# Folding two of the first batch's three sample tiles on TensorE, in float32

## The chip, the cores and the metric

The kernel runs on one core of a Trainium2 chip. The metric is the time of one execution on the device, in microseconds (us). The engines of the core work side by side, each on its own stream of instructions: TensorE (PE in the profile; its weight loads are PEld), VectorE (DVE), ScalarE (ACT), GpSimd (POOL) and SyncE (SP), which here only starts transfers.

## The reference

A batch `x` of shape 4 x 3072 x 256 goes through a Fourier transform over both its axes, of which the real part is kept. Then follow a gated layer whose gate mixes the 3072 tokens with a 3072 x 3072 matrix, and a second gated layer.

```python
X = np.fft.fft(np.fft.fft(x, axis=1), axis=2)
x = X.real.astype(np.float32)
h = np.maximum(x @ w_in, 0.0)
u, v = h[..., :512], h[..., 512:]
v_n = (v - mean(v)) / np.sqrt(var(v) + 1e-06)
v_s = np.einsum('ts,bsd->btd', w_spatial, v_n) + b_spatial[None, :, None]
x = (u * v_s) @ w_out
gate = 1.0 / (1.0 + np.exp(-(x @ w_gate)))
return (gate * (x @ w_val)) @ moe2_w_out
```

## The kernel before, in words

Float32 accuracy is made of float32r matmuls: an operand is split into a high part (a cast on ScalarE) and a low part (a subtraction on VectorE), and `mm3` (lines 259 to 261) forms high x high, high x low and low x high, three matmuls for one product, and leaves low x low out.

The program has three stages. The first transforms the four batches one after the other and multiplies by `w_in`; the second is the large product with `w_spatial`, and the third the last layer. The order on every engine is written out by hand (`manual_schedule`): an engine gets its instructions in the order in which the Python code issues them.

The change is in what precedes the first batch's transform, the opening. There

- three sample tiles of batch 0 (m = 0, 1, 2), each in two halves `xt` of 512 KB (`xts[m, hd]`), are folded: rows that the transform's symmetry pairs are added and subtracted over three levels, from 16 x 64 values per partition down to 8 x 64. `fold_x` and `folds` (lines 356 to 379) do one half tile with twelve VectorE instructions. The result, `fo[m]`, is split into `fh` and `fl` (`split_fold`);
- `w_in` comes as 64-bit words in four pieces. `convert` makes float32 of two pieces at a time: `from64_first` on ScalarE (lines 275 and 276, two instructions a piece), `from64_rest` on VectorE (lines 281 to 299), a cast to `wih` on ScalarE (line 463), and, in the returned `rest`, the low part `wil` on VectorE (line 468);
- `first_weights` multiplies the converted pieces by the transform over the model dimension: 16 matmuls `psg`, the first on `wih`, the second on `wil`; `take` brings them to `gc` and `g3`;
- `mirror_samples` (lines 537 to 541) makes the samples `sps` of special rows: once for batch 0 and the last column, once for batches 1 to 3;
- `take_nyquist` (lines 581 and 582) makes `nts`, of which `own_samples` (line 599, ScalarE) makes `nt`, that the first unit's fourth matmul (line 628) needs.

In program order the opening is: fold tile 2; convert pieces 0 and 1; exchange rows of tile 2; fold half 0 of tile 0; `wil`; `first_weights(1)`; fold half 1 of tile 0; `mirror_samples` for batch 0; split tile 0; `take`; convert pieces 2 and 3; fold half 0 of tile 1; `wil`; `first_weights(0)`; transform of tiles 2 and 0; fold half 1 of tile 1; split tile 1; and the rest of the first unit. From there on GpSimd folds the tiles of batches 1 to 3 while TensorE works on the batch before.

Of the kernel before, what the change touches and what calls it, by code (L numbers as in the profile page):

```python
# [9 lines left out]
F32 = mybir.dt.float32  # L10
# [5 lines left out]
ALU = mybir.AluOpType  # L16
# [3 lines left out]
B, S, D = 4, 3072, 256  # L20
# [4 lines left out]
P = 128  # L25
# [112 lines left out]
def _masks():  # L138
    m = np.zeros((P, 3 + B), np.float32)
    for b in range(B):  # L140
        m[32 * b : 32 * b + 3, 3 + b] = 1.0
        m[32 * b + 2, 0] = -1.0
        m[32 * b + 1, 1] = -1.0
    m[64:68, 2] = -1.0
    return m
# [8 lines left out]
def _slots():  # L154
    r = _samples()
    rows = [r, 768 - r, 1536 - r, 768 + r, 3072 - r, 2304 + r, 1536 + r, 2304 - r]
    return np.stack(rows, 1) % S


def layouts(x, moe_w_in, moe_w_spatial, moe_b_spatial, moe_w_out, moe2_w_gate, moe2_w_val, moe2_w_out):  # L160
    tau = _token_order()
    slots = _slots()
    dup = [3, 4, 6, 7]

    def halves(xb):

        o = np.zeros(xb.shape[:-1] + (2, P), np.float32)
        o[..., 0, :] = xb[..., :P]
        o[..., 1, 1:] = xb[..., : D // 2 : -1]
        return o  # L170

    g = x[:, slots]
    g[:, 0, dup] = 0.0
    xh = halves(g).reshape(B, 3, P, 8, 2, 2, 64).transpose(0, 1, 5, 2, 3, 4, 6)
    gn = g[..., D // 2].reshape(B, 3, P, 8).transpose(2, 3, 1, 0)
    fam = np.array([384, 1152, 1920, 2688])
    sp = halves(x[:, fam])
    xs = np.zeros((P, B + 1, 2, P), np.float32)
    for at in (0, 32, 64):
        xs[at : at + 4, :B] = sp.transpose(1, 0, 2, 3)  # L180
        for b in range(B):
            for c in range(3):
                xs[at : at + 4, B, 0, 32 * b + c] = x[b, fam, D // 2]
    w = moe_w_spatial[tau][:, tau]
    wt = w.reshape(6, 512, 24, P).transpose(0, 3, 2, 1)
    wg, wv = (w.reshape(2, P, 12, P) for w in (moe2_w_gate, moe2_w_val))
    arrays = {
        "xh": xh,
        "xn": gn.reshape(P, 8, 3 * B),
        "xs": xs,  # L190
        "w_in": moe_w_in.reshape(2, P, DFF).transpose(1, 0, 2),
        "wt": wt,
        "bt": moe_b_spatial[tau].reshape(1, S),
        "w_out": moe_w_out.reshape(4, P, DM).transpose(1, 0, 2).reshape(P, 2, 512),

        "w_b": np.concatenate(
            [
                np.stack([wg[0], wg[1], wv[1], wv[0]]).transpose(1, 2, 0, 3).reshape(P, 12, 512),
                moe2_w_out.reshape(12, P, DM).transpose(1, 0, 2).reshape(P, 6, 512),
            ],  # L200
            axis=1,
        ),
    }
    arrays.update(_constants())
    arrays["spc"] = _special_constants()
    arrays["fd"] = _dft_d()
    arrays["masks"] = _masks()

    arrays = {k: np.ascontiguousarray(v) for k, v in arrays.items()}
    return {k: v.view(np.uint64) if v.dtype == np.float64 else v for k, v in arrays.items()}, tau  # L210
# [27 lines left out]
def tile_kernel(ctx: ExitStack, tc: tile.TileContext, t: dict, out: bass.AP):  # L238
    nc = tc.nc
# [62 lines left out]
    def pool(stack, name, bufs, side="left", **kw):  # L302
        return stack.enter_context(tc.tile_pool(name=name, bufs=bufs, side=side, reuse_waits="tile", **kw))
# [4 lines left out]
    ln_all = lnp.tile([P, 320], F32, name="ln_all")  # L308
# [12 lines left out]
    ps_w = pool(ps0, "ps_w", 6, space=PSUM)  # L321
# [48 lines left out]
    def load_x(b, m, hd, p=xp, bufs=2):  # L370
        xt = p.tile([P, 8, 2, 64], F32, tag="xt", name="xt", bufs=bufs)
        nc.sync.dma_start(xt, t["xh"][b, m, hd])
        return xt

    def fold_x(eng, xt, fo, hd, et):
        at = slice(hd * 64, hd * 64 + 64)
        eng.tensor_tensor(out=et, in0=xt[:, :, 0, :], in1=xt[:, :, 1, :], op=ALU.add)  # L377
        eng.tensor_tensor(out=xt[:, :, 0, :], in0=xt[:, :, 0, :], in1=xt[:, :, 1, :], op=ALU.subtract)  # L378
        folds(eng, [(0, et, fo[:, 0, :, at]), (1, xt[:, :, 0, :], fo[:, 1, :, at])])

    def new_fo():
        return fop.tile([P, 2, 4, P], F32, tag="fo", name="fo")

    def new_et(p=xp):
        return p.tile([P, 8, 64], F32, tag="et", name="et", bufs=1)
# [15 lines left out]
    def fft(fold, b, unit, q, e=0, ps=None, tiles=(0, 1, 2), end=True, early=False):  # L401

        n = R3 if unit == 3 and q == 0 else H
        begin = ps is None
        if begin:

            ps = ps_w.tile([P, 512], F32, tag="pa", name="psf") if early else ps_f.tile([P, 512], F32, tag="f", name="psf")
        ops = []
        if unit < 2:
            for i, (m, s) in enumerate(((e, q), (e, 1 - q), (2, (e + q) % 2))):
                ops.append((m, s, [c[:, e, i, :] for c in cc["c1"]]))
        else:
            name = ("c2", "c3")[unit - 2] + "pq"[q]
            for m in range(3):
                ops.append((m, unit, [cc[name][i][:, m, :] for i in range(2)]))
        sp = {(0, 0): SP_P1, (0, 1): SP_Q1, (2, 1): SP_Q2, (3, 0): SP_P3}.get((unit, q)) if begin else None  # L420
        for i in tiles:
            m, s, c = ops[i]
            fh, fl = fold[m][:2]
            last = end and sp is None and i == tiles[-1]
            mm3(ps[:, :n], (fh[:, q, s, :], fl[:, q, s, :]), c, begin and i == tiles[0], last, skip_group_check=e > 0)
        if sp is not None:
            nc.tensor.matmul(out=ps[:, :n], lhsT=sps[:, b, q, :], rhs=spc[:, sp : sp + n], start=False, stop=end)
        return ps, n
# [16 lines left out]
    fo = {m: new_fo() for m in (2, 0, 1)}  # L445
    xts = {}
# [7 lines left out]
    def convert(two):  # L454

        new = lambda: tmp.tile([P, 512], F32, tag="cv", name="cv", bufs=5)
        values = from64_rest(from64_first([words[i] for i in two], new), new())
        parts = []
        for i, value in zip(two, values):
            c, h = pieces[i]  # L460
            sl = slice(h * 512, h * 512 + 512)
            hi, lo = (x[:, c, sl] for x in wih)
            nc.scalar.copy(hi, value)
            parts.append((hi, lo, value))

        def rest():
            for hi, lo, value in parts:
                nc.vector.tensor_tensor(out=lo, in0=value, in1=f(hi), op=ALU.subtract)

        return rest  # L470

    def fold0(m, hd):
        fold_x(nc.vector, xts[m, hd], fo[m], hd, new_et())


    xts[2, 0] = load_x(0, 2, 0)
# [1 line left out]
    words = [load_w(0), load_w(1)]  # L478
    xts[0, 0] = load_x(0, 0, 0)
    xts[0, 1] = load_x(0, 0, 1, tmp, RING)  # L480
    fd = tmp.tile([P, 2 * 512 + 256], F32R, name="fd")
    nc.gpsimd.dma_start(fd, t["fd"])
    xn = tmp.tile([P, 8, 3 * B], F32, name="xn")
# [11 lines left out]
    fold0(2, 1)  # L495
    xts[1, 0] = load_x(0, 1, 0)
    xts[1, 1] = load_x(0, 1, 1, tmp, RING)
    rest = convert([0, 1])
    words += [load_w(2), load_w(3)]
    fold = {2: split_fold(fo[2], 2, None)}  # L500
    fold0(0, 0)
    rest()

    def first_weights(h):
# [24 lines left out]
        return take  # L529

    take = first_weights(1)
    fold0(0, 1)

    es = tmp.tile([P, B + 1, P], F32, name="es")

    def mirror_samples(bs):
        nc.vector.tensor_tensor(out=es[:, bs], in0=xs[:, bs, 0, :], in1=xs[:, bs, 1, :], op=ALU.add)
        nc.vector.tensor_tensor(out=xs[:, bs, 1, :], in0=xs[:, bs, 0, :], in1=xs[:, bs, 1, :], op=ALU.subtract)
        for q, e in ((0, es[:, bs]), (1, xs[:, bs, 1, :])):
            nc.scalar.copy(sps[:, bs, q, :], e)  # L540
            nc.vector.scalar_tensor_tensor(
                out=sps[:, bs, q, :], in0=f(sps[:, bs, q, :]), scalar=masks[:, 2:3], in1=e, op0=ALU.mult, op1=ALU.add
            )
# [16 lines left out]
        nc.vector.tensor_tensor(out=lo, in0=src, in1=f(hi), op=ALU.subtract)  # L560
        fold_n[m] = (hl[:, 0:1], hl[:, 1:2])

    fold0(1, 0)
    rest()
    load_table("c2", {"c2p": (3, H), "c2q": (3, H)})
    take = first_weights(0)
    sums = [fft(fold, 0, 3, q, tiles=(2, 0), end=False, early=True) for q in range(2)]
    fold0(1, 1)
    spread(2)
    spread(0)  # L570
    fold[1] = split_fold(fo[1], 1)
# [3 lines left out]
    spread(1)  # L575
    pq = [take_fft(*sums[q], q) for q in range(2)]
    load_table("c1", {"c1": (2, 3, H)})
    mirror_samples(slice(1, B))

    def take_nyquist(ps, n, unit):  # L580
        nc.scalar.copy(nts[unit], ps[:, :n])
        nc.vector.scalar_tensor_tensor(
            out=nts[unit], in0=f(nts[unit]), scalar=masks[:, 0:1], in1=ps[:, :n], op0=ALU.mult, op1=ALU.add
        )

    for unit in (3, 2):
        take_nyquist(*fft(fold_n, B, unit, 0, early=True), unit)
    s0.close()
    stp = pool(r0, "stp", 2, "right")
    vp = pool(r0, "vp", 9, "right")  # L590
# [540 lines left out]
    p, i, c = leaves[-1]  # L1131
# [83 lines left out]
    for n, leaf in enumerate(leaves[:-1]):  # L1215
        p, i, c = leaf
        base = 4 * (n % 2)
        ps = [banks(base + d) for d in range(4)]
# [33 lines left out]
    ps = [banks(base + d) for d in range(4)]  # L1252
# [196 lines left out]
```

## Time and profile before

| | |
|---|---|
| time, median of 3 runs | 2888.73 us (2887.54 to 2888.93) |
| the profiled execution's own time | 2888.82 us |
| its span, first to last instruction | 2886.7 us |
| mean granted TensorE clock | 0.995 |
| TensorE busy | 2823.3 us (98% of the span) |
| VectorE busy | 2018.2 us (70%) |

The profile is that of one execution. The span leaves out some 2 us of the execution's own time. TensorE's share of busy time is an average: it says nothing of the opening, in which TensorE mostly waits.

### The profile page before, as it was taken

How to read it: one execution, taken by the hardware profiler on the slowest of the kernel's cores; microseconds unless marked ns; L12 is line 12 of the kernel's file. 1: busy time of each engine (PE TensorE's matmuls, PEld its weight loads, DVE VectorE, ACT ScalarE, POOL GpSimd, SP SyncE). 2: the span in 40 equal slices, each digit the busy share in tenths (PEclk: the TensorE clock that was granted, in tenths of full speed). 3: DMA queues.
4: the chain of work that ended last, by engine and by line, in shares of the span. 5: the costliest groups of instructions: out<-in, count | busy, mean ns of one | idle time of the engine just before them, and what ended most of it. 6: DMA issues, size and time to landing. Idle time of an engine off the chain costs nothing.

```text
span 2886.7 us, 34266 instructions
## 1 busy us (share of the span) xinstructions
PE 2823.3 (98%) x12550; PEld 2349.2 (81%) x12550; DVE 2018.2 (70%) x3001; ACT 1426.1 (49%) x2267; POOL 212.1 (7%) x333
## 2 busy tenths in 40 slices
PE   4999999999999999999999999999999999999999
PEld 4888788888888888888888888888888888888887
DVE  7777766797766567578667476866676666776665
ACT  4777444244334244344334333656556565565655
POOL 2883000001000000000000000000000000000000
PEclk9999999999999999999999999999999999999999
DMA  6777867798666678478776474200000000000000
GB/s 232 281 274 273 293 212 236 257 316 275 237 210 224 225 249 289 159 268 286 251 245 241 155 275 144 87 30 30 30 15 15 30 30 30 15 15 30 30 15 15
DMA packets 148180, 470.76 MB, mean 163 GB/s; under 512 B 16797, under 2 KB 18333, under 8 KB 147628
## 3 DMA queue, kind: packets, MB, share of 16 engines
q1 hardware_dynamic: 140540, 434.88, 43.9%
q0 software_dynamic: 4016, 21.11, 1.9%
q10 hardware_dynamic: 3456, 12.58, 1.1%
q8 instruction: 98, 1.61, 0.2%
q14 instruction: 70, 0.57, 0.1%
HBM read 385.94 MB, written 82.58 MB: 162 GB/s over the span
## 4 chain that ended last, share of the span: by engine, by line
PE 91%; POOL 3%; DVE 2%; ACT 1%; issue 1%; DMA 1%; ACTq 0%; SPq 0%; POOLq 0%; DVEq 0%
PE bank L259 30%; PE bank L260 30%; PE bank L261 30%; POOL et L377 0%; POOL xt L378 0%; DMA xt<-in_xh 0%; POOL fo L362 0%; POOL xt L360 0%; PE psf L259 0%; DMA u_d<-tu 0%; PE psv L260 0%; PE psv L259 0%; PE psv L261 0%; PE psu L261 0%; PE psu L260 0%
## 5 line engine op out<-in xcount | busy, mean ns | idle before, releaser
L259 PE MATMUL bank<-wh,vh 128*128 128x512 f32 x2016 | 785.7, 390 | 5.7 <-DVE ln_all L708 5.7
L261 PE MATMUL bank<-wh,vl 128*128 128x512 f32 x2016 | 785.5, 390 | 0.0
L260 PE MATMUL bank<-wl,vh 128*128 128x512 f32 x2016 | 785.4, 390 | 0.0
L828 ACT CAST wh<-st 128x1024 fp32r<-128x1024 f32 x252 | 264.4, 1049 | 507.1 <-PE bank L261 389.0
L831 DVE TENSOR_TENSOR wl<-st,wh 128x1024 fp32r<-128x1024 f32 x252 | 309.7, 1229 | 235.5 <-ACT wh L828 230.6
L259 PEld LDWEIGHTS bank<-wh,vh 128*128 128x128 f32 x2016 | 379.2, 188 | 85.2 <-DVE ln_all L708 6.4
L261 PEld LDWEIGHTS bank<-wh,vl 128*128 128x128 f32 x2016 | 379.1, 188 | 79.0
L260 PEld LDWEIGHTS bank<-wl,vh 128*128 128x128 f32 x2016 | 379.2, 188 | 78.6
L259 PE MATMUL bank<-x,wgh 128*128 128x512 f32 x673 | 262.4, 390 | 0.5 <-ACT t L1344 0.4
L1332 DVE TENSOR_TENSOR t<-t,bank 128x512 f32<-128x512 f32 x144 | 99.0, 688 | 233.7 <-PE bank L261 233.7
L260 PE MATMUL bank<-x,wgh 128*128 128x512 f32 x673 | 261.8, 389 | 0.0
L261 PE MATMUL bank<-x,wgl 128*128 128x512 f32 x673 | 261.8, 389 | 0.0
L1353 DVE TENSOR_TENSOR gl<-s,gh 128x512 fp32r<-128x512 f32 x288 | 199.5, 693 | 57.7 <-ACT gh L1351 44.3
L259 PE MATMUL bank<-gh,wv 128*128 128x512 f32 x576 | 224.2, 389 | 0.8 <-ACT gh L1346 0.8
L260 PE MATMUL bank<-gl,wv 128*128 128x512 f32 x576 | 224.2, 389 | 0.2 <-DVE gl L1353 0.2
L261 PE MATMUL bank<-gh,wv 128*128 128x512 f32 x576 | 224.1, 389 | 0.0
L826 DVE TENSOR_TENSOR st<-st 128x1024 f32<-128x1024 f32 x180 | 220.7, 1226 | 3.4 <-DMA st<-in_wt 3.1
L1323 ACT ACTIVATE s<-s 128x512 f32<-128x512 f32 x144 | 91.0, 632 | 153.1 <-DVE s L1322 153.1
L809 ACT ACTIVATE st<-st,ln_all 128x512 f32<-128x512 f32 x168 | 127.6, 808 | 66.3 <-DMA st<-v_d 52.4
L259 PEld LDWEIGHTS bank<-x,wgh 128*128 128x128 f32 x673 | 126.3, 188 | 28.6 <-ACT s L1320 0.9
L261 PEld LDWEIGHTS bank<-x,wgl 128*128 128x128 f32 x673 | 126.3, 188 | 26.2
L260 PEld LDWEIGHTS bank<-x,wgh 128*128 128x128 f32 x673 | 126.3, 188 | 26.0
(236 smaller groups left out, 4467.5 us busy)
## 6 DMA issues: line engine op xcount, KB each, us to landing
st<-in_wt SPq DMA_DIRECT2D x432, 512.0 KB, 5.4
st<-v_d SPq DMA_DIRECT2D x144, 512.0 KB, 5.3
u<-u_d SPq DMA_DIRECT2D x96, 256.0 KB, 3.5
u_d<-tu SPq DMA_DIRECT2D x48, 384.0 KB, 3.7
v_d<-tv SPq DMA_DIRECT2D x69, 256.0 KB, 3.7
xt<-in_xh SPq DMA_DIRECT2D x24, 512.0 KB, 4.1
x_d<-x ACTq DMA_DIRECT2D x24, 512.0 KB, 6.1
raw<-x_d SPq DMA_DIRECT2D x24, 512.0 KB, 4.0
```

What stands on the lines that cost most here:

```text
L259: nc.tensor.matmul(out=ps, lhsT=w[0], rhs=x[0], start=first, stop=False, **kw)
L260: nc.tensor.matmul(out=ps, lhsT=w[0], rhs=x[1], start=False, stop=False, **kw)
L261: nc.tensor.matmul(out=ps, lhsT=w[1], rhs=x[0], start=False, stop=last, **kw)
L809: nc.scalar.activation(st[:, k, :], st[:, k, :], AF.Identity, scale=scale[:, at], bias=shift[:, at])
L826: nc.vector.tensor_tensor(out=tiles[0], in0=tiles[0], in1=tiles[1], op=op)
L828: nc.scalar.copy(hl[0], tiles[0])
L831: lows.append(lambda: nc.vector.tensor_tensor(out=hl[1], in0=tiles[0], in1=f(hl[0]), op=ALU.subtract))
L1323: nc.scalar.activation(s1, s1, AF.Sigmoid)
L1332: nc.vector.tensor_tensor(out=g["t2"], in0=g["t2"], in1=g["b"], op=ALU.add)
L1353: nc.vector.tensor_tensor(out=l, in0=s, in1=f(h), op=ALU.subtract)
```

## The change

Tiles 0 and 1 of batch 0 are no longer folded by `fold_x`. `fold0_sums` has TensorE add the rows: for each half tile 8 matmuls in float32, of 256 columns each, with the identity or its negative as weights and `xt` as it came (not split) as the moving operand. They form the first two additions of the fold, in two PSUM tiles `psx`. ScalarE copies half of each of them to `fo`. `fold0_rest` does the remaining levels with six VectorE instructions of 128 x 256 for the whole tile. The identity and its negative are a new input of 128 KB, loaded by ScalarE's own DMA queue into `ln_all`, which is not yet in use then. `mirror_samples` for batches 1 to 3 moves behind `take_nyquist`.

```diff
+    arrays["ident"] = np.concatenate([np.eye(P), -np.eye(P)], 1).astype(np.float32)
...
+    ident = ln_all[:, : 2 * P]
+    signs = {0: ((1, 1), (1, 1)), 1: ((1, -1), (-1, 1))}
...
+    def fold0_sums(m):
+
+        sums = [ps_w.tile([P, 4, P], F32, tag="pa", name="psx") for _ in range(2)]
+        for hd in range(2):
+            xt = xts[m, hd]
+            for q, ps in enumerate(sums):
+                terms = [(half, k) for half in range(2) for k in range(2)]
+                for half, k in terms:
+                    w = ident[:, :P] if signs[q][half][k] > 0 else ident[:, P:]
+                    nc.tensor.matmul(
+                        out=ps[:, :, hd * 64 : hd * 64 + 64],
+                        lhsT=w,
+                        rhs=xt[:, 4 * half : 4 * half + 4, k, :],
+                        start=(half, k) == (0, 0),
+                        stop=(half, k) == (1, 1),
+                        skip_group_check=hd > 0,
+                    )
+        for q, ps in enumerate(sums):
+            nc.scalar.copy(fo[m][:, q, 2:4, :], ps[:, 2:4, :])
+        return sums
+
+    def fold0_rest(m, sums):
+
+        tt = nc.vector.tensor_tensor
+        e = new_et().rearrange("p s d -> p (s d)").rearrange("p (q s d) -> p q s d", q=2, s=2)
+        for q, ps in enumerate(sums):
+            plus, minus = (e[:, q], fo[m][:, q, 0:2, :])[:: -1 if q else 1]
+            tt(out=plus, in0=ps[:, 0:2, :], in1=fo[m][:, q, 2:4, :], op=ALU.add)
+            tt(out=minus, in0=ps[:, 0:2, :], in1=fo[m][:, q, 2:4, :], op=ALU.subtract)
+        to = fo[m].rearrange("p q s d -> p (q s) d")
+        tt(out=to[:, 2:8:5, :], in0=e[:, :, 0, :], in1=e[:, :, 1, :], op=ALU.subtract)
+        tt(out=to[:, 3:7:3, :], in0=e[:, :, 0, :], in1=e[:, :, 1, :], op=ALU.add)
...
+    nc.scalar.dma_start(ident, t["ident"])
     fd = tmp.tile([P, 2 * 512 + 256], F32R, name="fd")
...
+    sums = fold0_sums(0)
     rest = convert([0, 1])
     words += [load_w(2), load_w(3)]
     fold = {2: split_fold(fo[2], 2, None)}
-    fold0(0, 0)
+    fold0_rest(0, sums)
     rest()
...
     take = first_weights(1)
-    fold0(0, 1)
+    sums = fold0_sums(1)
...
-    fold0(1, 0)
+    fold0_rest(1, sums)
     rest()
...
-    fold0(1, 1)
     spread(2)
...
-    mirror_samples(slice(1, B))
...
     for unit in (3, 2):
         take_nyquist(*fft(fold_n, B, unit, 0, early=True), unit)
+    mirror_samples(slice(1, B))
     s0.close()
```

Line numbers of the kernel after are one higher than before up to line 470, and 38 or 39 higher behind that.

ScalarE at the start of the program, before (in brackets what an instruction waits for, an engine or a DMA queue):

```order
L275 ACT_TABLE_LOAD
L275 ACTIVATE cv<-words 128x512 [waits DMAHW2_49]
L276 ACTIVATE cv<-words 128x512
L275 ACTIVATE cv<-words 128x512 [waits DMAHW3_49]
L276 ACTIVATE cv<-words 128x512
L463 CAST wih<-cv 128x512 [waits DVE_49] x2
```

The same place after:

```order
L518 DMA ln_all<-in_ident 128x256
L497 ACT_TABLE_LOAD
L497 COPY fo<-psx 128x256 [waits PE_49] x2
L276 ACTIVATE cv<-words 128x512 [waits DMAHW3_49]
L277 ACTIVATE cv<-words 128x512
L276 ACTIVATE cv<-words 128x512 [waits DMAHW4_49]
L277 ACTIVATE cv<-words 128x512
L464 CAST wih<-cv 128x512 [waits DVE_49] x2
```

The two copies of tile 0's sums, which wait for TensorE, now stand ahead of the first conversion of `w_in`.

ScalarE behind the cast of tile 2, before:

```order
L396 CAST fh<-fo 128x1024 [waits Activation_49]
L540 CAST sps<-es 128x2x128 [waits DVE_49]
L540 CAST sps<-xs 128x2x128 [waits DMAHW0_49,DVE_49]
L254 CAST fh<-fo 128x1024
L521 CAST gh<-psg 128x512 [waits PE_49] x2
```

The same place after:

```order
L397 CAST fh<-fo 128x1024 [waits Activation_49]
L497 COPY fo<-psx 128x256 [waits PE_49] x2
L579 CAST sps<-es 128x2x128 [waits DVE_49]
L579 CAST sps<-xs 128x2x128 [waits DMAHW1_49,DVE_49]
L255 CAST fh<-fo 128x1024
```

The copies of tile 1's sums stand ahead of the samples `sps`, of tile 0's cast and of `take`; on TensorE these sums stand between `first_weights(1)` and `first_weights(0)`.

ScalarE at the end of the opening, before:

```order
L434 CAST ph<-psf 128x384 [waits PE_49]
L540 CAST sps<-es 128x3x128 [waits DVE_49]
L540 CAST sps<-xs 128x3x128 [waits DVE_49]
L581 CAST nt_144<-psf 128x386 [waits PE_49]
L581 CAST nt_143<-psf 128x384 [waits PE_49]
L599 ACTIVATE nt<-nt_144,masks 128x386 [waits DMAHW6_49,DMAHW7_49,DMASW0_49,DVE_49]
```

The same place after:

```order
L435 CAST ph<-psf 128x384 [waits PE_49]
L618 CAST nt_144<-psf 128x386 [waits PE_49]
L618 CAST nt_143<-psf 128x384 [waits PE_49]
L579 CAST sps<-es 128x3x128 [waits DVE_49]
L579 CAST sps<-xs 128x3x128 [waits DVE_49]
L637 ACTIVATE nt<-nt_144,masks 128x386 [waits DMAHW0_49,DMAHW7_49,DMASW0_49,DVE_49]
```

The samples of batches 1 to 3 have moved behind the two casts of `nts`; they still stand ahead of `nt`.

## Rows read from the trace of the kernel before

**Rows 1.** The page's first part: busy time, share of the span, instructions.

```profile
PE 2823.3 (98%) x12550; PEld 2349.2 (81%) x12550; DVE 2018.2 (70%) x3001; ACT 1426.1 (49%) x2267; POOL 212.1 (7%) x333
```

**Rows 2.** Stretch, length, busy PE, PEld, DVE, ACT, POOL; granted clock, DMA share, GB/s.

```profile
0.00:17.40 17.40, 0.00 (x0) 0.00 (x0) 12.65 (x37) 4.34 (x6) 4.64 (x12) 1.00 0.92 339
17.40:53.20 35.80, 18.41 (x70) 15.04 (x71) 34.41 (x84) 15.32 (x33) 8.33 (x10) 0.81 0.61 235
53.20:249.00 195.80, 184.34 (x934) 165.55 (x934) 143.40 (x392) 150.55 (x314) 148.03 (x233) 1.00 0.72 255
249.00:298.80 49.80, 38.01 (x177) 32.77 (x175) 38.42 (x109) 35.81 (x71) 17.24 (x32) 0.88 0.84 318
298.80:2886.70 2587.90, 2582.54 (x11373) 2135.84 (x11373) 1789.33 (x2383) 1220.05 (x1846) 33.87 (x48) 1.00 0.44 151
```

**Rows 3.** The chain that ended last, in the opening: start, duration, piece.

```profile
0.75 3.73 DMA xt<-in_xh
...
26.51 0.95 ACT fh L254
```

**Rows 4.** Timeline of VectorE: start, duration, line, operation, [idle before, releaser].

```profile
11.21 0.75 DVE L281 TENSOR_SCALAR cv<-cv 128x512 f32<-128x512 f32 x2
11.88 0.75 DVE L284 TENSOR_SCALAR cv<-cv 128x512 uint32<-128x512 uint32 x2
...
17.30 0.68 DVE L377 TENSOR_TENSOR et<-xt 128x512 f32<-128x512 f32 x1
...
18.63 0.42 DVE L360 TENSOR_TENSOR et<-et 128x256 f32<-128x256 f32 x1
18.96 0.42 DVE L360 TENSOR_TENSOR xt<-xt 128x256 f32<-128x256 f32 x1
...
20.65 1.28 DVE L468 TENSOR_TENSOR wil<-cv,wih 128x512 fp32r<-128x512 f32 x2
```

**Rows 5.** Timeline of ScalarE.

```profile
8.91 0.67 ACT L275 ACTIVATE cv<-words 128x512 f32<-128x512 f32 x1 [6.89 <-DMA words<-in_w_in]
9.48 0.66 ACT L276 ACTIVATE cv<-words 128x512 f32<-128x512 uint32 x1
10.57 0.67 ACT L275 ACTIVATE cv<-words 128x512 f32<-128x512 f32 x1 [0.42 <-DMA words<-in_w_in]
...
25.65 0.41 ACT L540 CAST sps<-es 128x256 fp32r<-128x256 f32 x1 [4.84 <-DVE es L537]
```

**Rows 6.** Timeline of GpSimd.

```profile
13.42 0.89 POOL L360 TENSOR_TENSOR xn<-xn 128x48 f32<-128x48 f32 x1 [11.47 <-DMA xn<-in_xn]
...
64.51 0.47 POOL L362 TENSOR_TENSOR fo<-et 128x128 f32<-128x128 f32 x1 [10.61 <-PE psf L261]
```

**Rows 7.** Timeline of TensorE.

```profile
21.38 0.79 PE L260 MATMUL psg<-wil,fd 128*128 128x512 f32 x1 [3.12 <-DVE wil L468]
...
22.40 0.63 PE L259 MATMUL psg<-wih,fd 128*128 128x512 f32 x1
22.83 0.63 PE L260 MATMUL psg<-wil,fd 128*128 128x512 f32 x1
...
24.44 0.40 PE L261 MATMUL psg<-wih,fd 128*128 128x512 f32 x1
...
25.81 0.39 PE L517 MATMUL psg<-wih,fd 128*128 128x512 f32 x1
26.04 0.39 PE L517 MATMUL psg<-wil,fd 128*128 128x512 f32 x1
...
41.43 0.79 PE L260 MATMUL psg<-wil,fd 128*128 128x512 f32 x1 [3.10 <-DVE wil L468]
```

**Rows 8.** Timelines of VectorE, TensorE and ScalarE at the end of the opening.

```profile
51.42 0.85 DVE L537 TENSOR_TENSOR es<-xs 128x384 f32<-128x384 f32 x1
...
53.03 0.33 PE L261 MATMUL psf<-c,fohl 128*128 128x384 f32 x1
...
55.40 0.62 ACT L599 ACTIVATE nt<-nt,masks 128x386 fp32r<-128x386 f32 x1 [0.80 <-DVE nt L582]
```

## The prediction

> **What bounds the kernel now.** I read the busy shares first: TensorE is busy for 98% of the span [rows 1]. Then the same by stretch, because the change touches only the first 56 us [rows 2]. Here the average falls apart. Until 17.40 us TensorE does nothing and VectorE is busy for 12.65 of 17.40 us, all the time from its first transfer's landing on. Until 53.20 us VectorE is busy for 34.41 of 35.80 us and TensorE for 18.41. From 53.20 us on TensorE leads: 184.34 of 195.80, then 38.01 of 49.80, then all but 5 of the last 2588 us. So the opening is bound by VectorE, and what it loses or gains moves everything behind it.
>
> The chain of waits says the same: it begins with the landing of the first `xt` [rows 3], runs along VectorE, crosses to ScalarE at 26.51 us (the cast `fh`, behind which `take` and the next conversion stand), returns to VectorE and reaches TensorE. VectorE's own timeline gives the pace. The conversion begins at 11.21 us, directly behind tile 2's folds; a half tile's fold then takes from 17.30 to 20.65 us, when `wil` follows [rows 4], and TensorE starts on `wil` at 21.38 us [rows 7].
>
> Does anything behind the opening swallow a shift of it? GpSimd's folds of batch 1 are the longest chain there, and GpSimd itself waits 10.61 us, until 64.51 us, for a transform matmul of this same sequence [rows 6]. It moves with TensorE. I take the shift of TensorE's sequence at the end of the opening as the change of the whole time.
>
> **What leaves.** Four half-tile folds of 3.35 us (17.30 to 20.65 us) leave VectorE: 13.4 us. In their place come twice six instructions of 128 x 256. Two such start 0.33 us apart [rows 4]; with a dependent pair and PSUM as a source I take 2.2 us for six, 4.4 us in all (bounds 2.0 and 2.6). VectorE gets 9 us lighter. Taken alone, that is a gain.
>
> **What is added: the price of the sums.** Each tile needs 16 matmuls of 256 columns in float32. The trace has no matmul whose operands are not cut to float32r before. From below: one pass costs half of what the 512-column rows cost. Those stand 0.43 us apart after a pause (22.40, 22.83 us; the 1.2 GHz level) and 0.23 us apart later in the burst (25.81, 26.04 us; 2.4 GHz) [rows 7], so 0.21 and 0.11 us. From above: this kernel makes a float32 product from float32r parts by `mm3`'s three matmuls and drops low x low; a product that keeps both operands whole has four part products, 0.86 and 0.45 us. I take four passes, since `mm3`, the only full product in these rows, lies next to that end. The burst that starts at 21.38 us has its first short matmul at 24.44 us; I let tile 0's burst, which also follows a pause, run 3.1 us at the low level too.
>
> The Trainium skill (FP8 and Floating Point Precision, section TensorE Precision Notes) says that a true float32 matmul makes four passes through the array. By that rule the sum is the one that I make below, by one pass it is the lower bound; no run here has shown it yet.
>
> **Where the copies stand.** The copies of the sums go to ScalarE, which works in its order. At 25.65 us its cast of `sps` had waited 4.84 us for VectorE [rows 5], and the conversion of pieces 2 and 3, which stands behind it, did not pass. The Trainium skill (PSUM — Partial Sum Buffer, section Engine vs sequencer instructions) states that ScalarE's and VectorE's queues are strict FIFO; this row agrees. So what stands behind the copies waits for TensorE.
>
> At the first place the copies of tile 0's sums stand ahead of the conversion's first ScalarE instructions, which ran at 8.91 us before, when the first words had landed. The sums need both halves of tile 0, which are sent for behind the words. The second words had landed by 10.57 us [rows 5] and `xn`, next in the queue behind tile 0, by 13.42 us [rows 6]; two equal transfers in between put the halves at 12.0 and 13.3 us. The identity's 128 KB, at 339 GB/s [rows 2], adds 0.4 us at most; I take 12.3 and 13.6 us. TensorE: 3.1 us at 0.86 us are 3.6 matmuls, the other 12.4 at 0.45 us take 5.6 us, so the sums end at 21.0 us. The second copy (0.41 us, as the 128 x 256 row of [rows 5]) frees ScalarE at 21.3 us. The four conversion instructions start 0.57 us apart (8.91, 9.48 us): the second `bits` starts at 22.45 and ends at 23.1 us. VectorE, idle since 11.5 us, then does the second of line 281 and reaches line 284 at 23.45 us instead of 11.88 us [rows 4]: **+11.6 us**.
>
> Some of it comes back between the conversion and `wil`: six instructions for 3.35 us of fold: **-1.15 us**. TensorE starts on `wil` at 31.8 us instead of 21.38.
>
> The second place: `first_weights(1)` takes 4.9 us (21.38 to 26.27 us) [rows 7], so to 36.7 us. Behind it tile 1's 16 sums, all at the high level: 7.2 us, to 43.9 us. The copies end at 44.3 us. Only then come the cast of `sps` (25.65 us before), of tile 0's `fh`, `take` and the conversion of pieces 2 and 3; that is 18.65 us late. VectorE, which has `es` done by 33 us, waits here for some 11 us: the fold of half 1 of tile 0, whose 3.35 us covered this stretch before, is gone, and the cover was no longer than that. Over the 10.45 us late already this adds **+8.2 us**.
>
> Ahead of the second `wil`, six instructions again stand for a fold: **-1.15 us**. TensorE's second burst starts at 59.0 us instead of 41.43. The fourth fold, half 1 of tile 1, ran beside this burst, and its removal is worth nothing: of TensorE's 18.41 busy us up to 53.20 us [rows 2], 5.05 are the first burst, 1.6 two single matmuls on `wih`, and the rest is all of the 11.8 us from 41.43 us on, without a gap that could close.
>
> At the end `mirror_samples` leaves its place ahead of `take_nyquist` on VectorE (from 51.42 us) [rows 8]. But ScalarE's `nt` (55.40 us) still stands behind its two casts, and the second of these needs `es` and `xs`. In the old time scale: the second `nts` needs the transform matmul that starts at 53.03 and ends at 53.4 us, cast to 53.9, VectorE to 54.4, `es` and `xs` to 55.4 (0.5 us each, one and a half times the 0.33 us of 256 columns; 0.85 us before, while GpSimd worked beside it), cast to 55.9. That is 0.5 us later than 55.40: **+0.5 us** (bounds -0.5 and +1.3).
>
> Other edits cost nothing: the loads of pieces 2 and 3 wait for the sums, but are needed 20 us later; `ident`'s issue lies in ScalarE's wait for words.
>
> **Sum.** 11.6 - 1.15 + 8.2 - 1.15 + 0.5 = **+18.0 us**. The profiled execution took 2888.82 us (span 2886.7), within 0.1 us of the median of 2888.73. So 2906.8 us, +0.62%.
>
> **The rivals.**
>
> One pass, or two. With 0.21 and 0.11 us tile 0's sums end at 15.7 us: line 284 comes 6.3 us late, `wil` 5.1 us, `first_weights(1)` ends at 31.4 us, the sums at 33.2, and `sps` is 7.9 us late; with -1.15 and +0.5 that is +7.2 us, 2896.0 us. Two passes, worked out in the same way, give +10.7, 2899.5 us. For: these operands are copied, not multiplied, and one part of the identity is zero. Against: an engine that looks at the type alone does the passes anyway. Chance 0.13.
>
> Dearer still. If all the sums run at the low level (13.7 us a tile), line 284 is 16.5 us late, the second place 30, the end 29.3: 2918 us. Weight loads that don't hide would lie between, at 2911 to 2915. Chance 0.12.
>
> Not slower, because the opening's delay is used up behind it. TensorE idles for 11.5 us between 53.20 and 249 us and 11.8 us up to 298.8 [rows 2]. If 12 us or more of that ended by something that does not move with the opening (a transfer that runs on its own), 18.0 us would shrink below 5.8, within 0.2% of before, which is about what a measurement of this kernel can tell from no change; at 18 us absorbed it decides for no change, 2889 us. For it speaks only that the idle is there. Against: each releaser that I find (`nt`, `pl`, the folds of the next batch) hangs on TensorE's own earlier steps, as GpSimd's 10.61 us does. Chance 0.05.
>
> Not slower, because the sums are cheap. Even matmuls that cost nothing leave tile 0's landing at 13.6 us ahead of the conversion: line 284 at 16.4 us, `first_weights(1)` ending at 29.7 us, two copies behind it to 30.4 us, where `sps` stood at 25.65: +4.75, less 1.15, plus 0.5 makes +4.1 us, 2892.9 us. Below 0.08 us a matmul this is within 0.2%; the cheapest row says 0.11. A gain would need the copies passed on ScalarE, against [rows 5]: then the folds' savings count, -2 to -5 us. Chance 0.04.
>
> **How the numbers follow.** Four passes as summed: 0.66, with 2903 to 2910 us from the landing (1 us), the low level's length (1.5 us) and the end. The predicted time is 2907 us. The range 2896 to 2914 leaves out no change (0.09), the dearest half of the dear case (0.06) and a little of the cheap one. Faster by over 0.2% (5.8 us): 0.03; within: 0.07; slower: 0.90.
>
> **What would show it.** Right: ScalarE idle from its start to 21 us, released by `psx`; VectorE idle from 11.5 to 22 us and again for some 11 us before the first `sps`; TensorE's `psx` stretches 8.7 and 7.2 us long; `wil`'s first matmuls near 31.8 and 59 us; the second stage starting near 317 us instead of 298.8. Wrong: `psx` matmuls 0.11 us apart; ScalarE converting words at 9 us; or the second stage starting at 299 us after a late opening.

## The result, and the profile after

The kernel after takes 2908.12 us (median of 5 runs, 2907.76 to 2909.58), the kernel before 2888.66 us beside it (5 runs): 19.5 us slower, a ratio of 1.007 with a 95% interval of 1.0059 to 1.008. The forecast was 2907 us.

The stretches of [rows 2] in the profile after, columns as there:

```profile
0.00:17.40 17.40, 5.03 (x16) 4.23 (x17) 6.72 (x24) 1.28 (x1) 3.61 (x13) 1.00 0.94 344
17.40:53.20 35.80, 16.96 (x65) 13.38 (x63) 18.25 (x37) 13.72 (x29) 1.90 (x2) 0.81 0.51 205
```

VectorE was busy for 12.65 and 34.41 us in these stretches; now it is for 6.72 and 18.25. It has less to do, but most of what is missing is waiting. ScalarE's timeline shows for whom:

```profile
19.33 0.37 ACT L497 COPY fo<-psx 128x256 f32<-128x256 f32 x1 [16.88 <-PE psx L488]
21.06 0.37 ACT L497 COPY fo<-psx 128x256 f32<-128x256 f32 x1 [1.35 <-PE psx L488]
21.33 0.67 ACT L276 ACTIVATE cv<-words 128x512 f32<-128x512 f32 x1
...
42.59 0.37 ACT L497 COPY fo<-psx 128x256 f32<-128x256 f32 x1 [10.21 <-PE psx L488]
44.32 0.37 ACT L497 COPY fo<-psx 128x256 f32<-128x256 f32 x1 [1.35 <-PE psx L488]
44.59 0.41 ACT L579 CAST sps<-es 128x256 fp32r<-128x256 f32 x1
```

The conversion of `w_in` starts at 21.33 us, where [rows 5] have it at 8.91, and the cast of `sps` at 44.59 instead of 25.65 us, each directly behind a copy that waited for `psx`. VectorE's timeline, against [rows 4]:

```profile
22.03 0.43 DVE L282 TENSOR_SCALAR cv<-cv 128x512 f32<-128x512 f32 x1 [10.16 <-ACT cv L276]
...
23.48 0.75 DVE L285 TENSOR_SCALAR cv<-cv 128x512 uint32<-128x512 uint32 x2
...
28.87 0.42 DVE L506 TENSOR_TENSOR et<-psx,fo 128x256 f32<-128x256 f32 x1
29.20 0.42 DVE L507 TENSOR_TENSOR fo<-psx,fo 128x256 f32<-128x256 f32 x1
...
31.00 1.29 DVE L469 TENSOR_TENSOR wil<-cv,wih 128x512 fp32r<-128x512 f32 x2
...
45.03 0.48 DVE L580 SCALAR_TENSOR_TENSOR sps<-sps,masks,es 128x256 fp32r<-128x256 f32 x1 [11.95 <-ACT sps L579]
```

It waits 10.16 us for the conversion's first step and 11.95 us for the cast of `sps`. The six instructions that replace a fold take 2.1 us (28.87 to 31.00). TensorE, against [rows 7] (a row with x32 holds the 32 records of one tile's 16 sums):

```profile
12.37 8.65 PE L488 MATMUL psx<-xt,ln_all 128*128 128x256 f32 x32 [12.37 <-DMA xt<-in_xh]
...
31.73 0.79 PE L261 MATMUL psg<-wil,fd 128*128 128x512 f32 x1 [1.88 <-DVE wil L469]
...
37.21 7.07 PE L488 MATMUL psx<-xt,ln_all 128*128 128x256 f32 x32
...
58.99 0.79 PE L261 MATMUL psg<-wil,fd 128*128 128x512 f32 x1 [1.89 <-DVE wil L469]
```

The two `wil` matmuls come at 31.73 and 58.99 us, 10.35 and 17.56 us later than before. At the end of the opening, TensorE before, TensorE after, and then VectorE and ScalarE after:

```profile
56.07 0.51 PE L628 MATMUL psv<-g,nt 128*128 128x512 f32 x1 [2.01 <-ACT nt L599]
```

```profile
75.43 0.50 PE L666 MATMUL psv<-g,nt 128*128 128x512 f32 x1 [3.43 <-ACT nt L637]
```

```profile
74.11 0.62 DVE L580 SCALAR_TENSOR_TENSOR sps<-sps,masks,xs 128x384 fp32r<-128x384 f32 x1
```

```profile
73.56 0.51 ACT L579 CAST sps<-xs 128x384 fp32r<-128x384 f32 x1
...
74.76 0.62 ACT L637 ACTIVATE nt<-nt,masks 128x386 fp32r<-128x386 f32 x1 [0.69 <-DVE sps L580]
```

The matmul that needs `nt` came at 56.07 us in the kernel before and comes at 75.43 now: 19.36 us late, 1.8 us more than the second `wil`. It follows a pause of 3.43 us, and the matmuls behind it fall to the low clock level (stretches of the profile after, columns as in [rows 2]):

```profile
76.00:77.00 1.00, 1.00 (x7) 0.86 (x5) 0.00 (x0) 0.88 (x2) 0.00 (x0) 0.93 0.00 0
77.00:81.00 4.00, 4.00 (x14) 3.52 (x13) 0.69 (x1) 1.34 (x3) 0.00 (x0) 0.59 0.01 2
```

The second stage begins 20.1 us late, at 318.91 us against 298.77 us before (first line before, second after):

```profile
298.77 0.80 PE L259 MATMUL bank<-wh,vh 128*128 128x512 f32 x1 [5.68 <-DVE ln_all L708]
...
318.91 0.79 PE L260 MATMUL bank<-wh,vh 128*128 128x512 f32 x1 [6.77 <-DVE ln_all L746]
```

The span is 19.2 us longer (2905.9 us). Nothing behind the opening used the delay up: the shift of TensorE's sequence there is the change of the time, within 1 us.

### The profile page after: what moved, and what is told of

Its sections match the earlier page's. It is cut to its first block, busy times and chain, and to the rows that moved or that the text cites. A ratio compares the mean times of both kernels' runs of the same rounds, so it can differ in the third digit from the quotient of the medians.

```text
span 2905.9 us, 34364 instructions
## 1 busy us (share of the span) xinstructions
PE 2837.9 (98%) x12614; PEld 2361.4 (81%) x12614; DVE 2008.6 (69%) x2965; ACT 1426.6 (49%) x2271; POOL 207.7 (7%) x333
## 4 chain that ended last, share of the span: by engine, by line
PE 92%; DVE 2%; ACT 2%; issue 2%; POOL 1%; DMA 1%; SPq 0%; ACTq 0%; POOLq 0%; DVEq 0%
PE bank L260 29%; PE bank L261 29%; PE bank L262 29%; PE psx L488 1%; DMA xt<-in_xh 1%; PE psf L260 0%; PE psf L262 0%; PE psf L261 0%; PE psv L261 0%; PE psv L262 0%; PE psv L260 0%; POOL et L378 0%; PE psu L262 0%; PE psu L261 0%; PE psu L260 0%
```

## The experiments

Beside the runs of the first four experiments the kernel before took 2888.11 us (median of 19 runs), beside the others 2888.45 us (19 runs).

**The copies where they are needed** (`e1_copies_late`). In the changed kernel the copies move from `fold0_sums` to the head of `fold0_rest`:

```diff
-        for q, ps in enumerate(sums):
-            nc.scalar.copy(fo[m][:, q, 2:4, :], ps[:, 2:4, :])
         return sums
...
     def fold0_rest(m, sums):
 
+        for q, ps in enumerate(sums):
+            nc.scalar.copy(fo[m][:, q, 2:4, :], ps[:, 2:4, :])
```

> The changed kernel with ScalarE's copies of the sums issued directly ahead of the VectorE instructions that need them, so behind the conversion of w_in. The queue theory: the conversion runs at 9 us again, VectorE loses its two long waits, the second wil matmul comes near 43 us (59.0 in the changed kernel, 41.4 before), and with some 2 us at the end of the opening the time is 2892 us (2890 to 2895), although the sums cost TensorE the same. The rival, that the sums' time on TensorE or the added transfer sets the loss wherever the copies stand: over 2900 us.

Measured: 2891.37 us (10 runs; ratio to before 1.0011, 1.0002 to 1.0021). 16.7 us of the 19.5 us are gone, though the sums cost TensorE what they did. TensorE's, VectorE's and ScalarE's timelines of this run:

```profile
12.72 8.75 PE L488 MATMUL psx<-xt,ln_all 128*128 128x256 f32 x32 [12.72 <-DMA xt<-in_xh]
...
41.20 0.80 PE L261 MATMUL psg<-wil,fd 128*128 128x512 f32 x1 [3.22 <-DVE wil L469]
...
58.22 0.79 PE L666 MATMUL psv<-g,nt 128*128 128x512 f32 x1 [3.43 <-ACT nt L637]
```

```profile
21.63 0.42 DVE L506 TENSOR_TENSOR et<-psx,fo 128x256 f32<-128x256 f32 x1 [3.73 <-ACT fo L501]
```

```profile
9.28 0.67 ACT L276 ACTIVATE cv<-words 128x512 f32<-128x512 f32 x1 [6.81 <-DMA words<-in_w_in]
```

The conversion starts at 9.28 us, and the second `wil` comes at 41.20 us, as in the kernel before. The copies' place in ScalarE's queue made most of the loss. But VectorE's 9 us bring nothing yet: it waits 3.73 us for tile 0's sums.

**Sums of one pass** (`e2_one_pass`). The sums read only the upper 16 bits of `xt` and of the identity, as bfloat16; the lower bits of tiles 0 and 1 are left out:

```diff
+            top = xt.rearrange("p a k d -> p a (k d)").bitcast(BF16).rearrange("p a (k d w) -> p a k d w", k=2, w=2)
...
-                        lhsT=w,
-                        rhs=xt[:, 4 * half : 4 * half + 4, k, :],
+                        lhsT=w.bitcast(BF16).rearrange("p (d w) -> p d w", w=2)[:, :, 1],
+                        rhs=top[:, 4 * half : 4 * half + 4, k, :, 1],
```

> The changed kernel, its sums on the upper 16 bits of xt and of the identity as bfloat16 (the lower bits of the first two tiles are left out): the same 32 matmuls of 256 columns, but of one pass. If the float32 price sets how long the copies hold ScalarE: sums of 3.4 and 1.9 us in place of 8.7 and 7.1, and 2897 us (2895 to 2899). If one record of 256 columns costs the same in either type: 2908 us. If the place in the queue alone costs it, whatever the price: 2905 us or more.

Measured: 2899.03 us (4 runs; 1.0038, 1.0023 to 1.0053). TensorE's timeline:

```profile
12.62 3.57 PE L490 MATMUL psx<-xt,ln_all 128*128 128x256 bf16 x16 [12.62 <-DMA xt<-in_xh]
...
32.94 1.99 PE L490 MATMUL psx<-xt,ln_all 128*128 128x256 bf16 x16
```

The 16 sums of tile 1 take 1.99 us in place of 7.07: a float32 sum costs 0.44 us, a one-pass sum 0.12 us. The price is thus worth 9 us of the 19.5, and the time lies at the upper edge of the range expected from it. The other 10 us stay even with cheap sums: some 3 of them are the move of the samples (the next two runs), and the rest goes with the place of the copies (`e1_copies_late`). (A row with x16 holds one tile's 16 sums, one record each; the expectation counts both tiles.)

**The samples back ahead of `take_nyquist`** (`e3_mirror_back`). In the changed kernel:

```diff
     load_table("c1", {"c1": (2, 3, H)})
+    mirror_samples(slice(1, B))
...
-    mirror_samples(slice(1, B))
     s0.close()
```

> The changed kernel with the samples of batches 1 to 3 back ahead of take_nyquist. From the trace of the changed kernel the move costs 1.8 us at the matmul that waits for nt and about 1 us more in the matmuls behind it, which run at the low clock level for 3 us: 2905.5 us (2904.5 to 2906.5). If it costs what the prediction put, 0.5 us: 2907.6. If the move is a gain: over 2908.5.

Measured: 2905.60 us (4 runs; 1.0061, 1.0046 to 1.0076). The interval overlaps that of the changed kernel, so the times alone would not carry this; the trace does:

```profile
59.16 0.80 PE L261 MATMUL psg<-wil,fd 128*128 128x512 f32 x1 [1.88 <-DVE wil L469]
...
72.79 0.51 PE L666 MATMUL psv<-g,nt 128*128 128x512 f32 x1 [0.57 <-ACT nt L637]
```

From the second `wil` to `nt`'s matmul it is 13.63 us, with a pause of 0.57 us; in the changed kernel 16.44 us and 3.43 us. The move costs 2.8 us there.

**The move alone** (`e4_mirror_only`). The kernel before, with only this move:

> The kernel before with only the samples of batches 1 to 3 moved behind take_nyquist. nt waits for the whole of mirror_samples (its memory was es and xs): PE's matmul of line 628 at 57.5 us instead of 56.1, and a pause of 3.6 us ahead of it: 2890 to 2891.5 us. By the prediction's 0.5 us: 2889.2. If the move relieves VectorE: under 2888.

Measured: 2891.80 us (10 runs; 1.0014, 1.0004 to 1.0023), 3.7 us slower than before and just above the expected range. TensorE's timeline:

```profile
57.80 0.49 PE L628 MATMUL psv<-g,nt 128*128 128x512 f32 x1 [3.43 <-ACT nt L599]
...
59.46 0.63 PE L261 MATMUL psv<-gh,pl 128*128 128x512 f32 x1
```

The same pause of 3.43 us, and again matmuls at the low level behind it (0.63 us long, 0.39 at the high level).

**What `nt` waited for** (`e8_own_memory`). In the changed kernel `xs` and `es` become the first tiles of their pool, so that `nt`, which is made after that pool has closed, lies on other memory:

```diff
     tmp = pool(s0, "tmp", 1, "right")
+    xs = tmp.tile([P, B + 1, 2, P], F32, name="xs")
+    es = tmp.tile([P, B + 1, P], F32, name="es")
...
-    xs = tmp.tile([P, B + 1, 2, P], F32, name="xs")
...
-    es = tmp.tile([P, B + 1, P], F32, name="es")
```

> The changed kernel with xs and es allocated first in their pool, so that the tile nt is no longer laid on their memory. If nt waited for the last VectorE instructions on es and xs because of that memory: nt starts right behind ScalarE's second cast, 0.7 us earlier, TensorE's pause is 2.7 us instead of 3.4, 2907 us (2906 to 2907.7); if the pause then no longer lowers the clock, 2906. If the wait was something else: 2908.1 and the same pause.

Measured: 2907.03 us (4 runs; 1.0065, 1.0048 to 1.0081). ScalarE's, VectorE's and TensorE's timelines:

```profile
76.07 0.51 ACT L578 CAST sps<-xs 128x384 fp32r<-128x384 f32 x1
76.48 0.61 ACT L636 ACTIVATE nt<-nt,masks 128x386 fp32r<-128x386 f32 x1
```

```profile
76.61 0.62 DVE L579 SCALAR_TENSOR_TENSOR sps<-sps,masks,xs 128x384 fp32r<-128x384 f32 x1
```

```profile
77.15 0.50 PE L665 MATMUL psv<-g,nt 128*128 128x512 f32 x1 [2.64 <-ACT nt L636]
...
78.89 0.39 PE L665 MATMUL psv<-g,nt 128*128 128x512 f32 x1
```

`nt` starts behind the cast without a wait, at 76.48 us, ahead of VectorE's last instruction on `xs` (76.61), for which it waited in the changed kernel. The matmuls behind the shorter pause stay at the high level. That the wait came from the memory is shown. The time is 1.1 us below that of the changed kernel; the two intervals against the kernel before overlap, so the time alone doesn't show a gain. (In this profile the first sums took 9.94 us instead of 8.65, so the whole opening lies later than in the profile of the changed kernel.)

**Both costs undone** (`e7_late_back`): the edits of `e1_copies_late` and `e3_mirror_back` together.

> The changed kernel with both of its costs undone: the copies directly ahead of what needs them, and the samples of batches 1 to 3 back ahead of take_nyquist. If the two costs add: 2891.4 less some 2.5 to 3.5, 2888.3 us (2887 to 2889.5), no better than the kernel before, since VectorE still waits 3.7 us for tile 0's sums and the conversion of pieces 2 and 3 still hangs on ScalarE behind take. If the 9 us of VectorE's time come out as time: 2880 us.

Measured: 2887.12 us (10 runs; 0.9996, 0.9987 to 1.0005): no different from before. TensorE's timeline:

```profile
41.66 0.79 PE L261 MATMUL psg<-wil,fd 128*128 128x512 f32 x1 [2.97 <-DVE wil L469]
...
54.77 0.50 PE L666 MATMUL psv<-g,nt 128*128 128x512 f32 x1 [0.57 <-ACT nt L637]
```

The second `wil` comes when it came before (41.43 us), and `nt`'s matmul 1.3 us earlier. The change without its two costs brings no gain clear of noise in this order of the program.

**Another order** (`e5_reordered`). With the sums on TensorE and the copies late, the opening is put in this order (cut short), and the identity goes on SyncE's queue ahead of tile 0:

```python
rest = convert([0, 1])
sums = fold0_sums(0)
mirror_sums()                      # all batches' es, xs and their casts
rest()
mirror_lows()
take = first_weights(1)
fold0_rest(0, sums)
sums = fold0_sums(1)
todo = from64_first([words[i] for i in (2, 3)], new)
...                                # exchange and casts of tiles 2 and 0
values = from64_rest(todo, new())
take()
...                                # casts to wih, then wil
fold0_rest(1, sums)
...                                # low parts of tiles 2 and 0
take = first_weights(0)
```

> The opening in another order, with the folds of tiles 0 and 1 on TensorE as in the changed kernel: the copies of the sums ahead of what needs them only; the samples of all batches in VectorE's wait for the first cast of w_in; the conversion of pieces 2 and 3 begun as soon as the first pieces are done, while TensorE sums tile 1; the identity on SyncE's queue. If the order was what took the gain: second wil matmul near 32 us instead of 41.4, nt's matmul near 46 to 48 us instead of 56.1, and 2879 us (2877 to 2883). The rival, that TensorE's 16 us of sums now bind: the second wil matmul at 36 us or later, over 2884 us.

Measured: 2876.47 us (4 runs; 0.996, 0.9945 to 0.9975): 12 us faster than the kernel before, 31.7 us faster than the changed one, and a little below the expected range. TensorE's timeline and the stretches up to its first wait for `nt`:

```profile
12.73 9.75 PE L488 MATMUL psx<-xt,ln_all 128*128 128x256 f32 x32 [12.73 <-DMA xt<-in_xh]
...
26.00 7.07 PE L488 MATMUL psx<-xt,ln_all 128*128 128x256 f32 x32
...
45.90 0.50 PE L684 MATMUL psv<-g,nt 128*128 128x512 f32 x1 [0.39 <-ACT nt L655]
```

```profile
17.40:45.50 28.10, 27.35 (x127) 23.14 (x126) 25.15 (x48) 17.70 (x38) 8.97 (x12) 1.00 0.81 322
```

TensorE goes through the opening almost without a pause (27.35 of 28.10 us), and `nt`'s matmul comes at 45.90 us instead of 56.07.

**The same order, folds on VectorE** (`e6_reordered_dve`): `fold0_sums` and `fold0_rest` of the run above become `fold0` again; no identity.

> The same new order, but all folds on VectorE as in the kernel before, no sums and no identity. If VectorE's 9 us matter once nothing waits for the sums: the 13.4 us of folds are back on the engine that binds, less what the new order alone saves: 2887 us (2884 to 2890), 6 us or more above the run with sums. The rival, that the order alone is the gain: within 2 us of the run with sums.

Measured: 2886.62 us (10 runs; 0.9994, 0.9985 to 1.0003). 10.2 us above the run with sums, and no different from the kernel before. TensorE's timeline:

```profile
45.12 0.44 PE L261 MATMUL psf<-c,fl 128*128 128x386 f32 x1 [2.54 <-DVE fl L397]
...
54.10 0.50 PE L682 MATMUL psv<-g,nt 128*128 128x512 f32 x1 [0.39 <-ACT nt L653]
```

TensorE waits for VectorE's `fl`. So neither this order alone nor the sums alone (`e7_late_back`) is a gain clear of noise; together they are, by about the 9 us that leave VectorE. Whether another order would be a gain with all folds on VectorE was not tried.

## Why the prediction was right, step by step

| step | predicted | measured in the trace |
|---|---|---|
| tile 0's sums end | 21.0 us | 21.0 us (12.37 + 8.65) |
| line 284 (285 after) late by | 11.6 us | 11.6 us (23.48 for 11.88) |
| six instructions for a fold | -1.15 us | -1.2 us (2.13 for 3.35) |
| first `wil` matmul | 31.8 us | 31.73 us |
| `first_weights(1)` | 4.9 us | 5.5 us (31.73 to 37.21) |
| tile 1's sums | 7.2 us | 7.07 us |
| cast of `sps` late by | 18.65 us | 18.94 us |
| second `wil` matmul | 59.0 us | 58.99 us |
| end of the opening | +0.5 us, bounds -0.5 and +1.3 | +1.8 us |
| second stage | 317 us | 318.91 us |

**The bound.** A shift of the opening is a shift of the whole. Right: the opening's 19.4 us came out as 19.2 us of span. That VectorE bound the opening held for what delays it; that time taken off it comes out as time did not hold (last paragraph of this section).

**The price of the sums.** Taken at four passes, from `mm3`'s products; measured 0.44 us a sum at the high level, 3.6 times the one-pass sum of `e2_one_pass`. The Trainium skill (FP8 and Floating Point Precision, section TensorE Precision Notes) names four passes for a true float32 matmul; the trace agrees as far as a ratio of 3.6 can. The rivals of one or two passes fall with it. The dearer rival, all sums at the low level at 13.7 us a tile, falls too: they took 8.65 and 7.07 us.

**The place of the copies.** Shown by `e1_copies_late`: the copies' place alone is worth 16.7 us. ScalarE did not let the conversion pass the waiting copies: it began at 21.33 us, and without the copies ahead of it, on the same loads, at 9.28.

**Not used up, and no cheap sums.** Both rivals on the other side fall. Between the opening and the second stage TensorE idles for some 26 us, against 23 before [rows 2], so nothing was swallowed there. And even at one pass the kernel was over 10 us slower than before; the +7.2 us that the prediction gave for one pass were too few.

**The step that was mis-sized** is the end of the opening, put at +0.5 us with a bound of +1.3: it was +1.8 us. The prediction had `nt` wait for ScalarE's second cast; it waited 0.69 us longer, for VectorE's last instruction on `xs`, because `nt` lies on that memory (`e8_own_memory`). It also left out that matmuls behind such a pause can run at the low level, as in the kernel after and in `e4_mirror_only`. The 1.3 us too little are most of the 1.5 us between the forecast sum of +18.0 us and the measured 19.5.

Inside the +1.8 us two larger amounts partly cancel. Against `e3_mirror_back` the move costs 2.8 us. Without it the way from the second `wil` to `nt`'s matmul is 13.63 us, 1.0 us less than the 14.64 before; the pause ahead of that matmul is 0.57 us instead of 2.01. The prediction put the removal of the fourth fold at nothing because it saw no gap in TensorE's work up to 53.20 us; the gap of 2.01 us stood just behind. That the missing fold is what shortened it is the likely reading, not shown by a run of its own.

**Luck.** That the second `wil` was met within 0.01 us is partly luck. `first_weights(1)` took 0.6 us more than put down, and smaller terms made up for it. The first sums alone differ by over 1 us between profiles (last section).

**What did not hold** is the sentence that VectorE's 9 us, taken alone, are a gain. `e7_late_back` shows none clear of noise (1.3 us, with an interval from 3.8 us faster to 1.4 us slower): with the copies out of the way, the next waits (VectorE for the sums, the second conversion behind `take`) put the second `wil` where it had been. Only the new order of `e5_reordered` turned the 9 us into time.

## What to carry to other kernels

Where an engine works in its order, a wait for a new result belongs directly ahead of the instruction that uses it; the same sums on TensorE cost 19.5 us or gained 12 us, depending on what stood behind the copies and on the order around them. Taking work off the busiest engine was worth nothing here until the program's order let that engine use the time: look for the next wait before counting the gain. And a tile that is made after a pool has closed may wait for the last reader of that pool's memory; moving such a reader to the end moves the wait too.

## What was not expected of the hardware

- A float32 matmul shows as two records: 32 of 128 x 256 for 16 instructions. They lie 0.22 us apart at the high level, where bfloat16 records of the same shape lie 0.12 us apart.
- VectorE's instructions with one operand in PSUM took what those with both in SBUF take: 0.42 us for 128 x 256, 0.33 us apart, in [rows 4] and in the profile after.
- The same 16 matmuls of tile 0's sums took 8.65, 8.75, 8.87, 9.49, 9.75 and 9.94 us in the profiles of the six kernels that have them in float32, where tile 1's took 7.07: the first matmuls behind the long wait run at the low level, for a time that differs by more than 1 us. That is as much as the smaller terms here.
- Behind the pause of 3.43 us in the kernel after the granted clock stayed at the high level for the first matmuls and then fell (0.59 from 77 to 81 us). Behind a pause of the same length in `e1_copies_late` it was at the low level from the first matmul on (0.50 from 58.2 us). Behind the pause of 2.64 us in `e8_own_memory` it stayed high (1.00 from 77 to 82 us).
